# Splitting a spectral kernel's token transforms by even and odd frequency, with ScalarE statistics, a shorter filter product and new pacing costs

## The chip, the core and the metric

One core of a Trainium2 chip runs the whole program. The engines are TensorE (PE, with its weight loads PEld), VectorE (DVE), ScalarE (ACT), GpSimd (POOL) and SyncE (SP, which issues the transfers). Each engine works through its own instructions in order; they meet at semaphores. The metric is the time of one execution on the device, in microseconds (us).

## What is computed

With x of 2048 tokens by 448 features, the output is x plus two branches on its layer norm: a spectral filter over both axes and a gated network of 1792 hidden columns.

```python
xn = _layernorm(x, axis=-1)
# A: X = rfft2(xn, axes=(-2, -1));  X = X * (w_r + 1j * w_i);  y = irfft2(X, s=(S, D))
# B: gate = xn @ W_gate;  up = xn @ W_up;  h = gate * (gate > 0) * up;  h @ W_down
return x + _A_ref(xn, A_w_r, A_w_i) + _B_ref(xn, B_W_gate, B_W_up, B_W_down)
```

S is 2048 and D is 448. Products are kept close to float32 by splitting each operand into a float16 high and low part: three passes (high by high, high by low, low by high) stand for one product.

## The kernel before

**The gated network** takes most of TensorE. Token sets q = 0, 2, 1, 3 of 512 tokens each meet the 14 hidden blocks in groups of 5, 5 and 4. One gate unit (`gu_unit`) is 20 full passes of 128x128 by 512 and a share of four half passes on 64 rows (`gu_halves`) that open the banks of the next unit. Behind it come `gu_relu` (ScalarE, L966), `gu_times` (VectorE, L970), `gu_hi` (ScalarE, L974) and `gu_lo` (VectorE, L978). A down unit (`dn_mm`) is 12 or 15 passes of 448 columns, seeded and read back by ScalarE.

**The spectral branch** runs in the background between these units. Tokens are n = 16 n1 + n2: a transform over n1 (128 points) by a matrix, and one over n2 (16 points) by butterflies on VectorE. Forward, for each pair (a, a + 8) of n2: `f_dft` (feature transform, 48 passes on 64 rows), eviction to `eo` by ScalarE (L479), `f_a` and `f_b` (VectorE), `f_hi` (ScalarE) and `f_lo` (VectorE) for the split, `f_sdft` (token transform, three passes of 128x128 by 464 for each n2), `f_y1` (first butterfly), then the later stages. The filter takes each block's mirror image by a transfer (`swap`), adds it (`pair`) and multiplies by the weights (`wmul`, four full-width and four half-width VectorE operations for two blocks: L621, L624, L626, L627, counting both). Backward, a round p = 0 to 7 for each pair (p, p + 8): `i_join` (L515 to L735), `i_swap`, `i_pair` (L661, L662), `i_mix` in two halves (L418 to L441), `i_hi` (ScalarE, L765), `i_lo` (VectorE, L770), `i_sdft` (12 passes of 128x128 by 128 for each n2), `i_pqhi` (ScalarE, L784), `i_pqlo` (VectorE, L787), `i_ddft` (48 passes on 64 rows, with x seeded by ScalarE, L798, and read back, L814).

**Statistics.** `ln_stats` takes mean and variance of a chunk of 128 tokens with VectorE's batch norm operations; chunks of sets 1 and 3 do so in the background (`ln_chunk`), then `ln_norm` on ScalarE, `ln_lo` on VectorE, and `ln_dma`, which transposes the tokens into the tile T of the set by a transfer.

**PSUM.** Two "gu" tiles of two banks, two "dn" banks, and two "fx" banks for all jobs of the spectral branch.

**What sets the order.** The opening is written out by hand (`OPENING`). After it, the list `bg` holds the background steps, each with a cost in us of VectorE time (`add`); `run_bg` takes as many at a unit as fit into a share of the unit's time (`room`, `load`), where `PE_US` and `V_US` give costs of TensorE jobs and of weight preparation. `offer` puts an `f_dft` or `i_ddft` up to stand behind a unit's half passes, if 6 us of units have gone by since; `force` places it if not. Passes of a job are tied together (`chained`), and later passes stand behind the last job taken that way (`state["bar"]`). A list scheduler then fixes each engine's order.

```python
    def offer(fn, *a):
        state["job"] = (state["at"], fn, a, 6.0)
```

## Time and profile before

| | before |
|---|---|
| median of 3 runs | 439.57 us (439.55 to 439.62) |
| span of the profiled execution | 438.4 us |
| TensorE busy | 430.9 us |
| VectorE busy | 371.2 us |
| ScalarE busy | 256.8 us |
| GpSimd busy | 36.4 us |
| transfers | 39.53 MB, mean 90 GB/s |

The profiled execution's own time is known as its span; the median of the timed runs is 1.2 us longer. A profile row gives the line, the engine, the operation, what is written and read, partitions by elements, the count, the busy time in us and the mean length in ns. Lengths of neighbouring operations of one engine overlap a little, so the distance from start to start in a timeline is the better price of one. A busy TensorE is not TensorE at its peak.

### The profile page before, as it was taken

How to read it: one execution, taken by the hardware profiler on the slowest of the kernel's cores; microseconds unless marked ns; L12 is line 12 of the kernel's file. 1: busy time of each engine (PE TensorE's matmuls, PEld its weight loads, DVE VectorE, ACT ScalarE, POOL GpSimd, SP SyncE). 2: the span in 40 equal slices, each digit the busy share in tenths (PEclk: the TensorE clock that was granted, in tenths of full speed). 3: DMA queues.
4: the chain of work that ended last, by engine and by line, in shares of the span. 5: the costliest groups of instructions: out<-in, count | busy, mean ns of one | idle time of the engine just before them, and what ended most of it. 6: DMA issues, size and time to landing. Idle time of an engine off the chain costs nothing.

```text
span 438.4 us, 8109 instructions
## 1 busy us (share of the span) xinstructions
PE 430.9 (98%) x3014; PEld 209.9 (48%) x3014; DVE 371.2 (85%) x916; ACT 256.8 (59%) x519; POOL 36.4 (8%) x72
## 2 busy tenths in 40 slices
PE   6999999999999999999999999999999999999997
PEld 2644544454444444444444444444554555554544
DVE  5998798999967999899999999698989978976213
ACT  5897494486357856625413675574565665756620
POOL 1140040033300040000000011000000000000000
PEclk9999999999999999999999999999999999999999
DMA  8769992042000363530402100020111121301112
GB/s 261 253 164 304 384 236 65 2 80 31 3 0 2 133 198 119 163 120 24 144 13 86 43 1 1 2 81 7 55 45 53 47 67 56 119 24 50 43 42 84
DMA packets 37720, 39.53 MB, mean 90 GB/s; under 512 B 17952, under 2 KB 32576, under 8 KB 37680
## 3 DMA queue, kind: packets, MB, share of 16 engines
q1 hardware_dynamic: 37680, 39.01, 29.3%
q8 instruction: 23, 0.38, 0.4%
q14 instruction: 17, 0.14, 0.1%
HBM read 24.25 MB, written 3.67 MB: 64 GB/s over the span
## 4 chain that ended last, share of the span: by engine, by line
PE 97%; ACT 1%; DMA 1%; DVE 0%; issue 0%; SPq 0%
PE gu L450 59%; PE dn L450 27%; PE fx L450 7%; PE dn L1034 1%; PE gu L1034 1%; DMA y<-in_xr 1%; ACT tt L330 1%; ACT junk L192 0%; PE fx L406 0%; PE fx L1034 0%; ACT y L321 0%; DVE bst L265 0%; ACT rs L282 0%; PE gu L384 0%; DVE xy L1013 0%
## 5 line engine op out<-in xcount | busy, mean ns | idle before, releaser
L450 PE MATMUL gu<-T,wt 128*128 128x512 f16 (+2 forms) x1250 | 269.6, 376 | 0.0
L450 PEld LDWEIGHTS <-wt 128*128 128x128 f16 (+1 forms) x1250 | 111.7, 97 | 141.4 <-issue 19.9
L450 PE MATMUL dn<-wdt,h 128*128 128x448 f16 x624 | 126.8, 353 | 0.0
L450 PEld LDWEIGHTS <-h 128*128 128x128 f16 x624 | 60.2, 98 | 57.3 <-issue 0.4
L974 ACT ACTIVATE h<-g 128x512 f16<-128x512 f32 x56 | 35.1, 626 | 61.4 <-DVE g L970 61.3
L970 DVE SCALAR_TENSOR_TENSOR g<-gu,g 128x512 f32<-128x512 f32 x56 | 38.5, 687 | 21.0 <-ACT g L966 20.9
L966 ACT ACTIVATE g<-gu 128x512 f32<-128x512 f32 x56 | 33.0, 590 | 35.4 <-PE gu L450 35.4
L1006 ACT ACTIVATE xy<-dn,dsc 128x448 f32<-128x448 f32 x44 | 27.6, 627 | 28.0 <-PE dn L450 27.9
L978 DVE TENSOR_TENSOR h<-g,h 128x512 f16<-128x512 f32 x56 | 38.4, 687 | 5.5 <-ACT h L974 5.5
L995 ACT ACTIVATE dn<-xy,dinv 128x448 f32<-128x448 f32 x44 | 27.8, 632 | 0.6
L195 POOL PARTITION_ALL_REDUCE wm<-wm x15 | 13.8, 929 | 170.5 <-ACT junk L192 170.5
L866 DVE SCALAR_TENSOR_TENSOR wt<-wst,wsc,wt 128x512 f16<-128x512 f32 x28 | 20.4, 747 | 3.8 <-ACT wt L862 3.8
L862 ACT ACTIVATE wt<-wst,wsc 128x512 f16<-128x512 f32 x28 | 19.2, 715 | 1.0 <-DVE wsc L202 0.9
L787 DVE SCALAR_TENSOR_TENSOR wf<-fx,wf 128x512 f16<-128x512 f32 x16 | 10.8, 690 | 8.9 <-ACT wf L784 8.9
L192 ACT ACTIVATE junk<-wst 128x512 bf16<-128x512 f32 x28 | 17.4, 623 | 1.3 <-DMA wst<-in_wgu 1.1
L784 ACT ACTIVATE wf<-fx 128x512 f16<-128x512 f32 x16 | 9.5, 597 | 9.8 <-PE fx L450 9.2
L814 ACT ACTIVATE xy<-fx,fsc 128x448 f32<-128x448 f32 x16 | 9.2, 629 | 9.4 <-PE fx L450 9.4
L527 DVE TENSOR_TENSOR y<-y,y 128x464 f32<-128x464 f32 x21 | 13.4, 639 | 0.2
L528 DVE TENSOR_TENSOR y<-y,y 128x464 f32<-128x464 f32 x21 | 13.4, 637 | 0.0
L265 DVE BATCH_NORM_STATS2 bst<-y 128x6 f32<-128x448 f32 x16 | 9.3, 621 | 4.4 <-DMA y<-in_xr 4.4
L770 DVE SCALAR_TENSOR_TENSOR vt<-wst,fsc,vt 128x464 f16<-128x464 f32 x16 | 10.5, 701 | 2.9 <-ACT vt L765 2.9
L450 PEld LDWEIGHTS <-vt 128*128 128x128 f16 x192 | 11.5, 98 | 1.9
(159 smaller groups left out, 489.5 us busy)
## 6 DMA issues: line engine op xcount, KB each, us to landing
wst<-in_wgu SPq DMA_DIRECT2D x28, 256.0 KB
wf<-in_wf SPq DMA_DIRECT2D x16, 232.0 KB
sw<-y SPq DMA_DIRECT2D x32, 114.2 KB
sw<-wst SPq DMA_DIRECT2D x16, 228.4 KB
y<-in_xr SPq DMA_DIRECT2D x16, 224.0 KB
xy<-in_x SPq DMA_DIRECT2D x16, 224.0 KB
out<-xy SPq DMA_DIRECT2D x15, 224.0 KB
wdst<-in_wd SPq DMA_DIRECT2D x14, 224.0 KB
```

The costliest lines, as they stand in the source:

```text
L192: A.activation(mt([128, 512], BF16, "junk")[:, 0:src.shape[-1]], src, AF.Square, scale=SQ, accum_out=acc)
L195: G.partition_all_reduce(o, i, 128, bass_isa.ReduceOp.add)
L450: r = P.matmul(*a, **k)
L527: V.tensor_tensor(t, a, b, op=OP.add)
L862: A.activation(w[:, 0:4, :], wst[f, g], AF.Copy, scale=wsc[f, g])
L866: V.scalar_tensor_tensor(w[:, 4:8, :], st, sc, w[:, 0:4, :], op0=OP.mult, op1=OP.subtract)
L966: last["A"] = A.activation(g1s[f, q], hps[f, q][:, 0, :], AF.Relu, scale=2.0 ** -22).ins
L970: last["V"] = V.scalar_tensor_tensor(g1, hps[f, q][:, 1, :], 2.0 ** -22, g1, op0=OP.mult, op1=OP.mult).ins
L974: A.activation(ht[f, q][:, 0, :], g1s[f, q], AF.Copy)
L978: V.tensor_tensor(h[:, 1, :], g1s.pop((f, q)), h[:, 0, :], op=OP.subtract)
L995: A.activation(dps[n2][:, 0:D], xy[n2], AF.Copy, scale=dinv[:, g:g + 1])
L1006: last["A"] = A.activation(xy[n2], dps[n2][:, 0:D], AF.Copy, scale=dsc[:, g:g + 1]).ins
```

## The change

- **Token transforms by even and odd.** Tokens are put in another order (`_tokens`), so that a partition block holds token halves n and n + 1024. `f_fold` on VectorE makes their sum and difference (the even and the odd frequencies) out of the banks of `f_dft`, with one half copied to SBUF by ScalarE first. `f_sdft` then takes 12 passes of 64 rows by 64 columns for a pair, and `i_sdft` 48 passes of 64 rows by 64 columns (128 weights). Backward, `i_part` (ScalarE) and `i_unfold` (VectorE) put the halves together ahead of `i_pqhi` and `i_pqlo`, which now is a plain subtraction.
- **fx** is one tile of two banks, not two tiles of one.
- **Statistics** of sets 1 and 3 go to ScalarE (`ln_sum`, `ln_var`); the last 64 columns of `ln_lo` are copied by ScalarE.
- **Filter product.** A third weight plane (a second copy of the imaginary part, one half negated by `wneg`) lets `wmul` take three full-width operations for a block.
- **Swaps** take four transfers for two, since the sine rows now stand in blocks of 32.
- **Costs** in the planner's tables are replaced, and `f_fold` and the forced `f_dft` stand ahead of `f_lo`.

```diff
+def _tokens():
+    b, p = np.arange(16)[None, :], np.arange(128)[:, None]
+    return (1024 * (b // 8) + 16 * (p % 64) + b % 8 + 8 * (p // 64)).reshape(-1)
...
+    def fx2():
+        return psum.tile([128, 2, 512], F32, name="fx", bufs=1)
...
-        V.bn_aggr(mv[q][:, j, :], bst.pop((q, j)))
+    def ln_sum(q, j):
+        A.activation(mt([128, 512], BF16, "junk")[:, 0:D], xr_t[q + 4 * j], AF.Copy, accum_out=mv[q][:, 0, j:j + 1])
+    def ln_var(q, j):
+        A.activation(mt([128, 512], BF16, "junk")[:, 0:D], xr_t[q + 4 * j], AF.Square, bias=mv[q][:, 1, j:j + 1],
+                     accum_out=mv[q][:, 2, j:j + 1])
...
-        for h in range(2):
-            with tc.high_priority(offset=400):
-                A.activation(F[:, 4 - 4 * h:8 - 4 * h].rearrange(...), banks[h][:, 0:2 * 4 * GW]..., AF.Copy,
+        t = fa[a] = free.pop(0)
+        with tc.high_priority(offset=400):
+            A.activation(t.rearrange("p (i s) c k -> p i (s c k)", i=2), ps[:, :, 0:4 * GW], AF.Copy,
+                         scale=2.0 ** -14)
+    def f_fold(a):
+        ps = fps.pop(a)[:, :, 4 * GW:8 * GW].rearrange("p i (x k) -> p i x k", k=KC)
+        for b in range(2):
+            V.scalar_tensor_tensor(F[:, b], ps, (-1.0) ** b * 2.0 ** -14, t, op0=OP.mult, op1=OP.add)
...
-    def f_sdft(n2):
-        for i, (a, b) in enumerate(((0, 0), (0, 1), (1, 0))):
-            mm(y, m[:, a, :], xh[:, b], start=(i == 0), stop=(i == 2), skip_group_check=True)
+    def f_sdft(a):
+        for i, (x, y) in enumerate(((0, 0), (0, 1), (1, 0))):
+            for k in range(2):
+                for b in range(2):
+                    p, q = slice(64 * k, 64 * k + 64), slice(64 * b, 64 * b + 64)
+                        m = chained(mm(ps[q, k, 0:XW], w[p, b, x], xh[p, y], start=(i == 0), stop=(i == 2),
...
+        for k2, x, t in ts:
+            V.tensor_tensor(t, x, ws[k2][:, 0, :, None, :].to_broadcast([128, NG, 2, KC]), op=OP.mult)
+        for k2, x, t in ts:
+            V.tensor_tensor(x, x, ws[k2][:, 1:3].rearrange("p c g k -> p g c k"), op=OP.mult)
+        for k2, x, t in ts:
+            V.tensor_tensor(t, t, x[:, :, ::-1], op=OP.add)
...
+    def i_sdft(p):
+        for b in range(2):
+            for g in range(4):
+                o = slice(64 * (2 * g + b), 64 * (2 * g + b + 1))
+                for i, (h, c) in enumerate(((0, 0), (0, 1), (1, 0))):
+                    for e in range(2):
+                        q = slice(64 * e, 64 * e + 64)
+                            m = chained(mm(ps[:, e, o], v[q, h, 128 * g:128 * (g + 1)], w[q, c],
+    def i_part(p):
+        A.activation(yu[p][:, 1], sps[p][:, 0], AF.Copy, scale=2.0 ** -14)
+    def i_unfold(p):
+        for b in range(2):
+            V.scalar_tensor_tensor(y[:, b], ps[:, 1], (-1.0) ** b * 2.0 ** -14, y[:, 1], op0=OP.mult, op1=OP.add)
+    def i_pqhi(p):
+        A.activation(t[:, 0], yu[p], AF.Copy)
+    def i_pqlo(p):
+        for b in range(2):
+            V.tensor_tensor(pgh[p + 8 * b][:, 1], y[:, b], pgh[p + 8 * b][:, 0], op=OP.subtract)
...
-    PE_US = {"f_dft": 0.85, "f_sdft": 0.59, "i_sdft": 0.65, "i_ddft": 0.82, "row_dft": 0.2}
+    PE_US = {"f_dft": 0.85, "f_sdft": 0.75, "i_sdft": 0.85, "i_ddft": 0.82, "row_dft": 0.2}
...
-    bf = (1.09, 1.74, 1.74, 1.74, 1.22, 1.74, 1.74, 1.74)
+    bf = (1.28, 2.07, 2.07, 2.07, 1.58, 2.07, 2.07, 2.07)
...
-        add(2.14, f_b, a)
+        add(3.02, f_b, a)
...
         if k < 7:
             add(0.0, force, f_dft, seq[k + 1], seq[k + 1] + 8)
+            add(1.27, f_fold, seq[k + 1])
         for n2 in (a, a + 8):
-            add(0.0, f_sdft, n2)
+            add(0.64, f_lo, a, n2)
+        add(0.0, f_sdft, a)
...
         if p:
-            both(0.6, i_pqlo, p - 1)
+            add(1.3, i_pqlo, p - 1)
             add(0.0, offer, i_ddft, p - 1, p + 7)
...
-            add(1.99, i_mix, p + 1, 0)
-    both(0.6, i_pqlo, 7)
+            add(1.28, i_pair, p + 1)
+        add(1.38, i_unfold, p)
+        add(0.0, i_pqhi, p)
+        if p < 7:
+            add(2.32, i_mix, p + 1, 0)
+    add(1.3, i_pqlo, 7)
...
-    V_US = {"w_scale": 0.2, "w_lo": 0.66, "wd_scale": 1.1, "wd_lo": 0.6}
+    V_US = {"w_scale": 0.33, "w_lo": 0.75, "wd_scale": 1.9, "wd_lo": 0.69}
...
-        c = 1.2 if units[i][0] == "gu" else 0.0
+        c = 1.37 if units[i][0] == "gu" else 0.0
```

**TensorE, fifth inverse round (p = 4).** In the program before, fx_4521 and fx_4534 are the two i_sdft of the round, fx_4644 and fx_4645 the banks of its i_ddft, gu_4601 a gate unit and dn_4746 a down unit; wf holds the split result between the two transforms. Before:

```order
L450 MATMUL fx_4534<-im_4204,vt_2350 128x128
L450 LDWEIGHTS wt_3560
L450 MATMUL gu_4601<-T1_64,wt_3560 128x512
...
L450 MATMUL dn_4746<-wdt_3713,h_4177 128x448
L450 LDWEIGHTS wf_4547
L450 MATMUL fx_4645<-idc_t_84,wf_4547 128x56
L450 LDWEIGHTS wf_4547
L450 MATMUL fx_4644<-idc_t_84,wf_4547 128x56
```

Gate and down passes stood between the two transforms. The same place in the changed kernel, where fx_4633 is i_sdft(4), fx_4808 is i_ddft(4), and gu_4782 and gu_4803 are a pair of gate units (line 495 is the line of every pass there):

```order
L495 LDWEIGHTS wt_3577
L495 MATMUL gu_4782<-T1_64,wt_3577 128x512
L495 LDWEIGHTS vt_2418
L495 MATMUL fx_4633<-im_4286,vt_2418 128x64
...
L495 LDWEIGHTS wf_4688
L495 MATMUL fx_4808<-idc_t_84,wf_4688 128x56
...
L495 LDWEIGHTS wt_3624
L495 MATMUL gu_4803<-T1_64,wt_3624 128x512
```

Before, 24 gate passes and 7 down passes stood between the two transforms of the round; now the last pass of i_sdft(4) is followed at once by the first of i_ddft(4), and the 20 full passes of gu_4803 stand behind it.

**VectorE at the same place.** Before, from the gate unit's operations to i_pqlo (L787) of the two n2 and the second half of i_mix:

```order
L978 TENSOR_TENSOR h_4577<-g1_4574,h_4577 128x512
L422 TENSOR_TENSOR wst_4239<-wst_4553 128x3x116
L423 TENSOR_TENSOR wst_4239<-wst_4553 128x3x116
L787 SCALAR_TENSOR_TENSOR wf_4547<-fx_4521,wf_4547 128x512
L787 SCALAR_TENSOR_TENSOR wf_4549<-fx_4534,wf_4549 128x512
L435 TENSOR_TENSOR wst_4239<-wst_4239 128x116
```

The two L787 came behind the whole first half of i_mix. In the changed kernel, where L853 is i_unfold, L463 to L468 the first half of i_mix and L863 i_pqlo:

```order
L1046 SCALAR_TENSOR_TENSOR g1_4925<-gu_4782,g1_4925 128x512
L1054 TENSOR_TENSOR h_4928<-g1_4925,h_4928 128x512
L853 SCALAR_TENSOR_TENSOR wf_4682<-fx_4633,wf_4682 128x512 x2
L463 TENSOR_TENSOR wst_4690<-wst_4331 128x2x232
L465 TENSOR_TENSOR wst_4690<-wst_4331 128x2x2x116
L467 TENSOR_TENSOR wst_4331<-wst_4690 128x3x116
L468 TENSOR_TENSOR wst_4331<-wst_4690 128x3x116
L863 TENSOR_TENSOR wf_4688<-wf_4682,wf_4688 128x512 x2
```

Two operations stood between i_sdft and the operands of i_ddft; now it is four, with the first half of the next round's i_mix between them and the gate unit's two ahead of them.

**ScalarE, statistics of the third token set.** In the changed kernel L302 is ln_sum, L308 ln_var, L313 the root, L391 the high part and L406 the copy of its last 64 columns. The rows from the last sum to the root:

```order
L302 ACTIVATE junk_984,ms_977<-y5_71 128x448
L1071 ACTIVATE dn_1447<-xy_61,dinv_92 128x448
L1042 ACTIVATE g1_1032<-gu_933 128x512
L308 ACTIVATE junk_987,ms_977<-y16_82,ms_977 128x448
L389 ACTIVATE y0_66<-y16_82,ms_977 128x448
...
L308 ACTIVATE junk_993,ms_977<-y5_71,ms_977 128x448
L503 ACTIVATE fx_878<-eps_93 128x1
L313 ACTIVATE rt_995<-ms_977,eps_93 128x4
```

These rows put all eight statistics passes and the four subtractions of the mean (L389) ahead of the root. Before, the first high part (L348) stood five rows behind the root (L282), and no statistics on this engine:

```order
L282 ACTIVATE rs_955<-mv_944,eps_93 128x4
L346 ACTIVATE y14_80<-y16_82,rs_955 128x448
L995 ACTIVATE dn_831<-xy_61,dinv_92 128x448
L497 ACTIVATE Xh_754<-eo_718 128x464
L497 ACTIVATE Xh_756<-eo_718 128x464
L348 ACTIVATE tt0_101<-y14_80,rs_955 128x448
```

The statistics have come from VectorE's queue into ScalarE's, ahead of the root, and the gate unit's L1042 now stands among them.

## The prediction

> **What bounds the kernel now.** I read the page first (span, busy times, chain), then the TensorE groups by shape, then timelines of one forward and one inverse round, engine by engine.

> ```profile
> span 438.4 us, 8109 instructions
> PE 430.9 (98%) x3014; PEld 209.9 (48%) x3014; DVE 371.2 (85%) x916; ACT 256.8 (59%) x519; POOL 36.4 (8%) x72
> PE 97%; ACT 1%; DMA 1%; DVE 0%; issue 0%; SPq 0%
> ```

> TensorE is the bound: 97% of the chain that ended last. After the opening it never stands, so every pass taken out shortens the run, and every new wait of TensorE lengthens it by its full length. VectorE is busy 371.2 of 438.4 us without being waited for. The first question is thus how much TensorE work goes, the second whether VectorE and ScalarE still deliver before TensorE asks.

> **TensorE work.** Rows of the groups by shape (count | busy, mean ns), then of the timeline (start, length, operation, count):

> ```profile
> L450 PE MATMUL fx<-im,vt 128*128 128x128 f16 x192 | 12.2, 219 | 0.0
> L450 PE MATMUL fx<-Xh,fm 128*128 128x464 f16 x48 | 11.2, 359 | 0.0
> L406 PE MATMUL fx<-id_t,tt 128*64 128x128 f16 x24 | 1.4, 246 | 0.0
> ...
> 68.97 0.82 PE L450 MATMUL fx<-fd_t,T 64*128 64x58 f16 x48
> 69.73 4.70 PE L450 MATMUL gu<-T,wt 128*128 128x512 f16 x22
> 74.27 1.34 PE L450 MATMUL fx<-Xh,fm 128*128 128x464 f16 x6
> 75.44 0.81 PE L450 MATMUL gu<-T,wt 128*128 128x512 f16 x3
> ...
> 354.16 1.50 PE L450 MATMUL fx<-im,vt 128*128 128x128 f16 x24
> 355.50 0.35 PE L450 MATMUL dn<-wdt,h 128*128 128x448 f16 x1
> ...
> 362.15 0.79 PE L450 MATMUL fx<-idc_t,wf 64*128 64x56 f16 x48
> 362.87 1.47 PE L450 MATMUL gu<-T,wt 128*128 128x512 f16 x6
> ```

> Start to start, the six forward passes of a pair cost 75.44 - 74.27 = 1.17 us (0.195 us per 464 columns, 0.42 ns a column), the 24 inverse ones 1.34 us. The 64-row passes show what halving does: 48 passes of 56 columns cost 0.72 us, 48 of 58 cost 0.76. Two run at once, so 24 x 56 x 0.42 ns = 0.56 us is work and 0.16 us the price of going in and out of the half-array form.
> - f_sdft becomes 12 passes of 64 rows by 64 columns, four at once: 3 x 0.195 + 0.16 = 0.75 us, saving 0.42 us a pair, 3.4 us in eight pairs. That column halves run together the trace shows only in the opening: 24 transposes of 128x64 are busy 1.4 us, 0.06 us each at a mean of 246 ns. Without it f_sdft costs 6 x 0.195 + 0.16 = 1.33 us and loses 1.3 us in all.
> - i_sdft becomes 48 passes of 64 rows and 64 columns, two at once: 24 x 64 x 0.42 ns + 0.16 = 0.80 us, saving 0.54 us, 4.3 us in eight.

> Together **-7.7 us**, with bounds of -3.0 (columns not together) and -8.5 (the 0.16 us shared with the neighbouring half passes).

> [...]

> **Vector and Scalar work.** Mean ns of the operations that come and go:

> ```profile
> L265 DVE BATCH_NORM_STATS2 bst<-y 128x6 f32<-128x448 f32 x16 | 9.3, 621 | 4.4 <-DMA y<-in_xr 4.4
> L627 DVE TENSOR_TENSOR y<-y,y 128x232 f32<-128x232 f32 x16 | 6.4, 397 | 0.0
> L556 DVE TENSOR_TENSOR y<-y,fx 128x464 f32<-128x464 f32 x8 | 5.0, 631 | 0.0
> L192 ACT ACTIVATE junk<-wdst 128x448 bf16<-128x448 f32 x14 | 7.9, 566 | 0.1
> L192 ACT ACTIVATION_READ_ACCUMULATOR junk<-wdst 128x1 f32 x14 | 2.6, 189 | 0.0
> ```

> VectorE gains f_fold (16 x 0.63 = 10.1 us) and 16 subtractions of 512 in i_pqlo (16 x 0.69 = 11.0, the length of the like L978 row below). It loses eight L265 (5.0 us), and the filter trades 32 half-width additions (12.7) for 16 full ones (10.1): +13 us of busy time, about 384 us. ScalarE gains 16 statistics passes of 0.566 + 0.189 us (12.1 us) and 8 copies of 1024 columns. In sum this costs nothing where TensorE is far behind; the cover is some microseconds in each round. Moving f_fold ahead of f_lo puts f_lo, and behind it f_sdft, after the f_dft of the next pair; 69.73 + 4.54 = 74.27 shows that TensorE does 4.5 us of gate work between these two, more than the copy and the two operations of f_fold (0.6 + 1.3), so nothing there. The single two-bank fx tile has the same cover. SP issues 56 more transfers:

> ```profile
> 208.86 0.88 SPq L609 DMA_DIRECT2D wf<-in_wf  x2
> 213.40 0.73 SPq L653 DMA_DIRECT2D sw<-y  x1
> ```

> A filter step would hold 8 issues of at most 0.73 and 4 of 0.44 us, 7.6 us, and SP stands from 209.7 to 213.4 between two steps; nothing, or where SP's queue fills, up to 1 us.

> **The place that decides: the fifth inverse round (p = 4).** The built order of the changed kernel puts i_ddft(4) straight behind i_sdft(4). Before, 24 gate and 7 down passes stood between them, about 6 us. i_ddft(4) reads what comes out of i_sdft(4) by way of ScalarE (i_part), VectorE (i_unfold), ScalarE (i_pqhi) and VectorE (i_pqlo), so TensorE must now wait for this whole chain. Its durations, from one round of before (VectorE, then ScalarE):

> ```profile
> 350.40 0.64 DVE L418 TENSOR_TENSOR wst<-wst 128x464 f32<-128x464 f32 x1
> ...
> 352.06 0.52 DVE L423 TENSOR_TENSOR wst<-wst 128x348 f32<-128x348 f32 x1
> 355.66 1.36 DVE L787 SCALAR_TENSOR_TENSOR wf<-fx,wf 128x512 f16<-128x512 f32 x2 [3.08 <-ACT wf L784]
> 356.94 0.27 DVE L435 TENSOR_TENSOR wst<-wst 128x116 f32<-128x116 f32 x1
> ...
> 359.32 0.39 DVE L515 SCALAR_TENSOR_TENSOR y<-y 128x232 f32<-128x232 f32 x1
> ...
> 359.94 0.69 DVE L970 SCALAR_TENSOR_TENSOR g<-gu,g 128x512 f32<-128x512 f32 x1
> 360.54 0.63 DVE L734 SCALAR_TENSOR_TENSOR wst<-y,y 128x464 f32<-128x464 f32 x1
> ...
> 361.64 1.31 DVE L770 SCALAR_TENSOR_TENSOR vt<-wst,fsc,vt 128x464 f16<-128x464 f32 x2
> 362.87 0.64 DVE L661 TENSOR_TENSOR wst<-wst,sw 128x464 f32<-128x464 f32 x1
> ...
> 363.97 0.69 DVE L978 TENSOR_TENSOR h<-g,h 128x512 f16<-128x512 f32 x1
> ...
> 355.03 1.27 ACT L784 ACTIVATE wf<-fx 128x512 f16<-128x512 f32 x2 [1.45 <-PE fx L450]
> ...
> 359.44 1.10 ACT L765 ACTIVATE vt<-wst,fsc 128x928 f16<-128x928 f32 x1 [0.47 <-DVE wst L441]
> 360.66 0.63 ACT L974 ACTIVATE h<-g 128x512 f16<-128x512 f32 x1
> 361.50 0.60 ACT L966 ACTIVATE g<-gu 128x512 f32<-128x512 f32 x1 [0.20 <-PE gu L450]
> ```

> Start to start on VectorE: first half of i_mix 352.06 - 350.40 + 0.44, less a hole of 0.1: 2.0 us; i_unfold 1.3 (as the two L787); second half 2.2 (356.94 to 359.32 has holes); i_join 0.62 + 1.10; gu_times 0.60, gu_lo 0.60; i_lo 1.23; i_pair 1.10; i_pqlo 1.2 (two like L978).

> *First wait.* Count from the end of the gate unit ahead of i_sdft(3). TensorE is through i_sdft(3), 37 gate passes of 0.216 (512 x 0.42 ns), i_ddft(3) and four half passes after 0.5 + 0.8 + 8.0 + 0.7 + 0.6 = 10.6 us, and asks for i_sdft(4). VectorE in its order: gu_times ends at 1.3 (0.65 behind ScalarE's L966), gu_lo at 2.65 (L974 between), i_unfold 3.95, i_mix 5.95, i_pqlo 7.15, second half 9.35, gu_times and gu_lo 10.55, i_join 12.25, i_lo(4) 13.5. TensorE waits 2.9 us.

> *Second wait.* i_sdft(4) ends at 14.3. VectorE: i_pair 14.6, gu_times 15.2; ScalarE's L974 15.9, then i_part 16.5, while gu_lo also ends at 16.5; i_unfold 17.8, i_mix 19.8 (ScalarE's i_pqhi, 1.10 x 1024/928 = 1.2 us, is done at 19.1), i_pqlo 21.0. TensorE stands from 14.3 to 21.0, 6.7 us. Queued behind the waiting pass are all later gate and down passes; SP and ScalarE are not held.

> Both: **+9.6 us**. Bounds: the bare chain, 0.6 + 1.3 + 1.2 + 1.2 = 4.3 us, and 12 us if VectorE enters the round 2.5 us late. I take 9.6, as the queues stand in the order.

> **The clock behind it.**

> ```profile
> 1.88 5.31 PE L1294 MATMUL dn<-bw 128*128 128x512 f16 x16 [1.88 <-POOL bw L1366]
> ...
> 433.83 1.31 PE L1034 MATMUL fx<-wdt,h 128*128 128x224 f16 x12
> ...
> 438.40:440.00 1.60, 0.00 (x0) 0.63 0.00 0
> ```

> TensorE's last pass ends at 433.83 + 1.31 = 435.14 us. In the window behind the span the granted clock (0.63, a mean over 1.6 us) has left 1.00; if it fell to one half, it did so at 438.8. So some 3.7 us of standing are enough, and 6.7 us fall into it. What a cold start costs the opening shows: 16 passes take 5.31 us and not 16 x 0.216 + 0.15 = 3.6: **+1.7 us**. Bounds 0 and, if it stays cold twice as long, 3.4.

> **The third token set.**

> ```profile
> 58.20 8.49 SPq L373 DMA_TRANSPOSE T<-tt  x4
> 78.60 1.67 PE L450 MATMUL gu<-T,wt 128*128 128x512 f16 x7
> ```

> The set's transposes are issued by 66.7 us and TensorE first needs them at 78.60: 12 us of cover. Now ScalarE does eight passes of 0.755 us (6.0 us), the squares wait for the mean on VectorE, and all four high parts (4 x 0.56) and low parts (4 x 0.6) stand behind the root; four issues of 1.4 us follow the first low part. That moves the last issue by 6.0 + 2.2 + about 3 of hand-overs, to 78, with the landing behind it. The cover is used up: **+1.0 us**, between 0 and 3.

> **Sum.** -7.7 + 9.6 + 1.7 + 1.0 = +4.6 us: the span goes from 438.4 to 443.0. The runs shown have a median of 439.57, 1.2 us over this execution's span; with the same 1.2 us I predict **444.2 us**.

> **Rivals.**
> - *VectorE is not behind at p = 4 (faster).* Then the first wait goes and the second shrinks to the bare chain of 4.3 us, too short a stand to bring the clock down for certain: 439.6 - 7.7 + 4.3 + 1.0 = 437.2. It decides at 5.8 us of waits in all: below that the change is faster by more than can be told from none (7.7 - 1.0 - 0.9). For it: before, VectorE itself waited 3.08 us ahead of L787 in such a round. Against: the round now asks 13.5 us of VectorE where TensorE gives 10.6. Chance 0.10.
> - *The clock holds* through the waits: 444.2 - 1.7 = 442.5. For it: 3.7 us is read off one fall at the end. Chance 0.13.
> - *VectorE is late elsewhere too*: 384 us of work in 443, with 8 weight halves and 2 statistics sets in the same queue; a second wait of 2 to 4 us makes 447. For it: the waits of L770 and L978 have little room. Against: no wait at 371 us of work. Chance 0.12.
> - *The change does not do what it says*: columns do not run together, saving 3.0: 448.9. Against: the opening's 0.06 us. Chance 0.04.
> - [...] Chance 0.03. [...]

> **How the numbers follow.** The forecast has 0.58; its own bounds run from 440 (both waits at their least, no late set) to 447. The range leaves out the ends of small chance, the first rival's 437.2 and 448.9: 439.0 to 447.5. About 0.2% (0.9 us) can be told from no change here. Faster by more: 0.11 (the first rival and a little of short waits); within: 0.08 (low ends of the forecast and of the clock's rival); slower: 0.81.

> **What would show it.** Passes of fx<-Xh,fm and fx<-im,vt: 0.75 and 0.80 us a pair in the timeline. A TensorE hole of about 3 us before, and one of 6 to 7 us behind, the fifth group of fx<-im,vt, near 365 us, ended by VectorE's i_pqlo; a window behind it with granted clock 0.5 for some 3.4 us; a hole of about 1 us ended by a DMA near 80 us. I am wrong if TensorE is still unbroken there, or if other holes add up to more.

## The result and the profile after

| | before | changed |
|---|---|---|
| median | 439.6 us (439.55 to 439.62) | 500.4 us (499.25 to 500.53) |
| span of the profiled execution | 438.4 us | 498.4 us |

The ratio is 1.138 (95% interval 1.136 to 1.139): 61 us slower, where 4.6 were forecast. The page of the changed kernel: the busy times, rows of the 40 slices of 12.5 us, and the chain that ended last by engine and by line.

```profile
span 498.4 us, 8711 instructions
PE 439.2 (88%) x3254; PEld 205.1 (41%) x3254; DVE 384.0 (77%) x908; ACT 269.4 (54%) x551; POOL 31.1 (6%) x72
...
PE   6999998899999999388669956994999995699997
...
DVE  6995877779999896565789568993998879986513
...
PEclk9999999999999999879889985999899999699999
...
DVE 33%; PE 25%; DMA 21%; ACT 9%; issue 5%; SPq 4%; POOL 1%; DVEq 0%; ACTq 0%; POOLq 0%
PE gu L495 14%; DMA sw<-y 12%; PE dn L495 7%; DMA y<-in_xr 3%; DVE g L1046 3%; DVE h L1054 3%; DMA wst<-in_wgu 2%; PE fx L495 2%; DMA xy<-in_x 2%; SPq L712 2%; DVE y L681 2%; DVE y L588 2%; DVE wt L942 1%; DVE y L587 1%; DVE y L603 1%
```

VectorE's busy time is what the prediction said (384), TensorE works in 88% of the span and not in 98%, and the chain is no longer TensorE's: it runs through VectorE and through a transfer, sw<-y, the swap of the filter. TensorE's row is nearly whole up to the sixteenth slice (two 8s between 75 and 100 us); the holes are in slices 17 to 28 (200 to 350 us), which is the filter and the start of the inverse rounds, and in 34 and 35, the fifth inverse round. TensorE's, then VectorE's and ScalarE's largest waits (line, what for: us in total, times, longest):

```profile
PE gu L495 <- DVE g L1046: 28.1, 7, 10.5
PE dn L495 <- ACT h L1050: 8.3, 1, 8.3
PE fx L495 <- ACT fx L874: 6.2, 1, 6.2
PE dn L495 <- ACT dn L1071: 2.4, 2, 1.3
PE fx L495 <- ACT xy L890: 2.4, 1, 2.4
PE gu L495 <- DMA T<-tt: 2.1, 1, 2.1
...
DVE y L719 <- DMA sw<-y: 29.0, 11, 3.7
...
ACT wf L675 <- DMA wf<-in_wf: 34.8, 9, 9.6
```

TensorE's two waits for fx (6.2 and 2.4) are those of the fifth inverse round, the one for T (2.1) is the late token set: the forecast's own. The first two rows, 36 us, are not in it. Behind them VectorE waits in `pair` (L719) for the swap, and ScalarE in `wneg` (L675) for the filter weights, and in both queues a gate unit's operations stand behind the waiting one. One place of each kind in the timeline (start, length, engine, operation; idle before it and what ended that), VectorE's first:

```profile
198.61 11.41 SPq L712 DMA_DIRECT2D sw<-y  x10
...
201.07 2.05 PE L495 MATMUL dn<-wdt,h 128*128 128x448 f16 x10
203.45 0.40 DVE L719 TENSOR_TENSOR y<-y,sw 128x232 f32<-128x232 f32 x1 [3.12 <-DMA sw<-y]
...
208.27 0.40 DVE L719 TENSOR_TENSOR y<-y,sw 128x232 f32<-128x232 f32 x1 [3.00 <-DMA sw<-y]
...
210.00 0.68 DVE L1046 SCALAR_TENSOR_TENSOR g<-gu,g 128x512 f32<-128x512 f32 x1
...
210.72 0.63 ACT L1050 ACTIVATE h<-g 128x512 f16<-128x512 f32 x1 [13.27 <-DVE g L1046]
...
211.40 2.04 PE L495 MATMUL dn<-wdt,h 128*128 128x448 f16 x5 [8.27 <-ACT h L1050]
...
233.25 0.40 ACT L675 ACTIVATE wf<-wf 128x232 f32<-128x232 f32 x1 [9.60 <-DMA wf<-in_wf]
233.55 0.58 ACT L1042 ACTIVATE g<-gu 128x512 f32<-128x512 f32 x1
```

SP needs 11.4 us for ten swap issues; VectorE gets two blocks 4.8 us apart, `gu_times` (L1046) stands behind both, and TensorE stands 8.3 us for its h. At 233 us it is ScalarE that waits, in `wneg`, with `gu_relu` (L1042) behind. Ahead of this SP had been issuing swaps without a pause. The same stretch of SP's queue in the kernel before (two transfers of 63 rows a swap; the first and the last of twelve issues in 9.7 us, 0.81 us each), then in the changed one (four of 31 and 32 rows):

```profile
173.15 0.87 SPq L653 DMA_DIRECT2D sw<-y  x1
...
182.16 0.71 SPq L654 DMA_DIRECT2D sw<-y  x1
```

```profile
185.92 24.10 SPq L712 DMA_DIRECT2D sw<-y  x24
```

24 issues in 24.1 us, 4.9 us a swap in its later part, while a single issue takes 0.6 us: SP waits between them. Its transfers raise eight semaphores in turn (in this trace each of the 275 behind the first eight raises that of the transfer eight issues back), and an issue waits for the landing of that one: those at 193.01, 195.71 and 197.98 us start behind landings at 192.99, 195.64 and 197.96 us. The trace holds the signals by which a transfer's landing is counted, and they point to the cause. By rows of the transfer: signals for each, and median time from the start of the issue to the last signal:

```
kernel           transfer                rows  signals  to the last signal
before           swap, filter              63       10  2.8 to 2.9 us
changed          swap, filter              31        2  7.5 us
changed          swap, filter              32       16  8.1 us
changed          swap, inverse             31        2  11.2 us
before           weights, two planes      128       16  3.4 us
changed          weights, two planes      128       16  6.3 us
```

A transfer of 31 rows has two signals where one of 32 has 16. In the six swaps from 185.92 us on, the last signals of the 31-row transfers come one behind another, 2.3 to 2.7 us apart (190.72, 192.99, 195.64, 197.96, 200.60 us and on), those of the 32-row transfers 0.2 us each behind them. The packets of the trace, one for each row, agree: of the first swap the first eleven start one behind another, each when the one ahead of it has ended, from 187.20 to 188.50 us; in the kernel before, of the 126 of the first swap's two transfers, 23 start within 0.25 us and 100 in the same time. This is read here as 31 rows going to one data engine, on which the 32-row transfers and the weights then queue too: the load issued at 210.39 us has its first signal at 212.57 us and its last at 218.57, 0.25 us behind the last of the swaps. That it is one engine, and why with 31 rows, is not shown: no packet of the trace says which engine carried it. An estimate from the trace: between 188 and 210 us a packet of 1856 bytes (one row) takes 78 ns in the median; a swap's 31 + 31 rows one behind another take 62 x 78 ns = 4.8 us, near the 4.9 us a swap above.

### The profile page after: what moved, and what is told of

The parts are those of the page before. It is cut to its first block, busy times and chain, and to the rows that moved or that the text cites. A ratio compares the mean times of both kernels' runs of the same rounds, so it can differ in the third digit from the quotient of the medians.

```text
span 498.4 us, 8711 instructions
## 1 busy us (share of the span) xinstructions
PE 439.2 (88%) x3254; PEld 205.1 (41%) x3254; DVE 384.0 (77%) x908; ACT 269.4 (54%) x551; POOL 31.1 (6%) x72
## 4 chain that ended last, share of the span: by engine, by line
DVE 33%; PE 25%; DMA 21%; ACT 9%; issue 5%; SPq 4%; POOL 1%; DVEq 0%; ACTq 0%; POOLq 0%
PE gu L495 14%; DMA sw<-y 12%; PE dn L495 7%; DMA y<-in_xr 3%; DVE g L1046 3%; DVE h L1054 3%; DMA wst<-in_wgu 2%; PE fx L495 2%; DMA xy<-in_x 2%; SPq L712 2%; DVE y L681 2%; DVE y L588 2%; DVE wt L942 1%; DVE y L587 1%; DVE y L603 1%
## 5 line engine op out<-in xcount | busy, mean ns | idle before, releaser
L495 PE MATMUL gu<-T,wt 128*128 128x512 f16 (+2 forms) x1250 | 278.6, 387 | 30.2 <-DVE g L1046 28.1
L495 PEld LDWEIGHTS <-wt 128*128 128x128 f16 (+1 forms) x1250 | 113.9, 99 | 181.1 <-issue 66.0
L495 PE MATMUL dn<-wdt,h 128*128 128x448 f16 x624 | 128.9, 356 | 12.3 <-ACT h L1050 8.3
L1046 DVE SCALAR_TENSOR_TENSOR g<-gu,g 128x512 f32<-128x512 f32 x56 | 38.3, 683 | 20.5 <-ACT g L1042 20.2
L1042 ACT ACTIVATE g<-gu 128x512 f32<-128x512 f32 x56 | 32.8, 586 | 17.3 <-PE gu L495 17.3
L719 DVE TENSOR_TENSOR y<-y,sw 128x232 f32<-128x232 f32 x16 | 6.4, 399 | 37.5 <-DMA sw<-y 29.0
L1082 ACT ACTIVATE xy<-dn,dsc 128x448 f32<-128x448 f32 x44 | 27.1, 623 | 10.6 <-PE dn L495 10.2
L1071 ACT ACTIVATE dn<-xy,dinv 128x448 f32<-128x448 f32 x44 | 27.4, 630 | 0.6
L675 ACT ACTIVATE wf<-wf 128x232 f32<-128x232 f32 x16 | 6.3, 394 | 34.9 <-DMA wf<-in_wf 34.8
L223 POOL PARTITION_ALL_REDUCE wm<-wm x15 | 9.0, 599 | 190.6 <-ACT junk L220 190.6
L534 DVE SCALAR_TENSOR_TENSOR eo<-fx,y 128x464 f32<-128x464 f32 x16 | 9.5, 631 | 8.3 <-ACT y L523 8.3
L823 ACT ACTIVATE vt<-wst,fsc 128x928 f16<-128x928 f32 x8 | 8.8, 1101 | 10.5 <-DVE wst L486 10.5
L874 ACT ACTIVATE fx<-xy,fsc 128x448 f32<-128x448 f32 x16 | 10.1, 628 | 7.9 <-DVE wf L853 7.8
L587 DVE TENSOR_TENSOR y<-y,y 128x464 f32<-128x464 f32 x21 | 13.3, 635 | 0.1
L588 DVE TENSOR_TENSOR y<-y,y 128x464 f32<-128x464 f32 x21 | 13.3, 634 | 0.1
L550 ACT ACTIVATE Xh<-eo 128x464 f16<-128x464 f32 x16 | 8.8, 594 | 8.2 <-DVE eo L486 8.0
```

The costliest lines, as they stand in the source:

```text
L495: r = P.matmul(*a, **k)
L587: V.tensor_tensor(t, a, b, op=OP.add)
L588: V.tensor_tensor(d, a, b, op=OP.subtract)
L1042: last["A"] = A.activation(g1s[f, q], hps[f, q][:, 0, :], AF.Relu, scale=2.0 ** -22).ins
L1046: last["V"] = V.scalar_tensor_tensor(g1, hps[f, q][:, 1, :], 2.0 ** -22, g1, op0=OP.mult, op1=OP.mult).ins
L1071: A.activation(dps[n2][:, 0:D], xy[n2], AF.Copy, scale=dinv[:, g:g + 1])
```

## The experiments

Theory A is the above. The rivals: B, the number of transfers and SP's time to issue them; C, the weights (three pairs of buffers for six single ones, a third plane loaded); D, VectorE has too much work.

**1. Wide swaps in the changed kernel.** Rows 0 and 32 are carried along, and GpSimd sets them to zero again.

```diff
-PAIRS = ((slice(1, 32), slice(33, 64)), (slice(33, 64), slice(1, 32)), (slice(64, 96), slice(96, 128)),
+PAIRS = ((slice(0, 32), slice(32, 64)), (slice(32, 64), slice(0, 32)), (slice(64, 96), slice(96, 128)),
...
         for o, i in PAIRS:
             nc.sync.dma_start(t[o], cur[key][i])
+        for r in (0, ROW): G.memset(t[r:r + 1], 0.0)
```

> The changed kernel with its swaps in transfers of 32 rows: the two of 31 rows (1 to 31 and 33 to 63) also carry rows 32 and 0, which GpSimd then sets to zero again; the number of transfers (four) and TensorE's order are as in the changed kernel. Theory A (a transfer of 31 rows is carried by one data engine, since its landing counts 2 signals where 63 rows count 10 and 32 rows 16; the swaps land in 7 to 8 us instead of 2.9, and SP, with eight transfers under way, stands): swaps land in about 3 us, TensorE's waits of 28 us for g and 8 us for h go, and the run takes what the forecast's other terms leave, 440 to 448 us. Rival B (the number of transfers and their issue time, 2.6 us a swap instead of 1.5): hardly better than the changed kernel, over 480. Rival C (three pairs of weight buffers instead of six single ones, an extra load a block): over 480, ScalarE still waits some 30 us for the weights. Rival D (VectorE has too much work, 384 us): over 470, TensorE waits for VectorE with the swaps landed.

454.5 us (454.39 to 455.55), ratio to the kernel before 1.034 (1.032 to 1.036). Its SP queue at the same place, the busy times, and TensorE's largest waits:

```profile
186.12 16.23 SPq L712 DMA_DIRECT2D sw<-y  x24
...
PE 429.2 (95%) x3254; PEld 203.1 (45%) x3254; DVE 383.3 (85%) x908; ACT 268.2 (59%) x551; POOL 61.0 (13%) x120
...
PE fx L495 <- ACT fx L874: 5.9, 1, 5.9
PE gu L495 <- DVE g L1046: 2.8, 3, 1.8
PE fx L495 <- ACT xy L890: 2.4, 1, 2.4
PE dn L495 <- ACT dn L1071: 2.4, 2, 1.4
PE gu L495 <- DMA T<-tt: 2.2, 1, 2.2
```

All swaps have 16 signals and land in 2.0 us (filter) and 2.2 us (inverse). The same number of issues now take 16.2 us. 46 of the 61 us are gone, and TensorE, VectorE and ScalarE work through the same instructions in the same order; 36 us of TensorE's waits became 3. Not all of the 46 us was waiting: TensorE's busy time for the same passes fell by 10.0 us (439.2 to 429.2), since 26.5 us of it ran at half clock in the changed kernel and 7.2 us here (the last section shows when the clock falls). A is right by far on what the landings cost. It leaves 454.5, above the 440 to 448 expected, so the forecast's other terms are some 10 us short; 5 to 7 answer that.

**2. Six wide transfers.** Rows 15 + 16 + 15 + 16 + 32 + 32, no zeroing.

```diff
+PAIRS = ((slice(1, 16), slice(33, 48)), (slice(16, 32), slice(48, 64)), (slice(33, 48), slice(1, 16)),
+         (slice(48, 64), slice(16, 32)), (slice(64, 96), slice(96, 128)), (slice(96, 128), slice(64, 96)))
```

> The changed kernel with each swap in six transfers of 15, 16 and 32 rows instead of four of 31 and 32: the same bytes, no zeroing, more transfers. Theory A: 15 rows go over several data engines, so the run comes near that with four wide transfers, within 5 us of it, although SP issues two more a swap (3.7 us a swap). Rival B (number of transfers): slower than the changed kernel, 505 to 530. Rivals C and D: as the changed kernel, 500.

461.6 us (1.050, 1.048 to 1.052); 15 rows have 16 signals and land in 2.1 us. Wide again, and far from the 505 to 530 of B; but 7 us behind the four, more than the 5 expected. ScalarE's wait for the weights is 31.9 us against 13.3 in experiment 1: the loads stand behind 4.0 us of issues a swap. B may have a small share, once there are six; how large is not shown, since the order of TensorE's passes is another from the filter on.

**3 and 4. The kernel before with four transfers a swap**, cut behind 33 rows (3, shown) or behind 32 (4, with 33 and 97 in CUT):

```diff
-        nc.sync.dma_start(t[1:64], cur[key][65:128])
-        nc.sync.dma_start(t[65:128], cur[key][1:64])
+CUT = ((1, 34), (34, 64), (65, 98), (98, 128))
...
+        for l, h in CUT:
+            nc.sync.dma_start(t[l:h], cur[key][(l + 64) % 128:(h + 63) % 128 + 1])
```

> The kernel before with each swap in four transfers (33, 30, 33 and 30 rows) instead of two of 63: prices the number of transfers alone. Theory A: landing near 3 us, 439.5 to 442. Rival B: SP's issue time, 24 x 1.0 us more, shows as 450 or more. Rivals C and D: 440.

> The kernel before with each swap in four transfers of 32 and 31 rows: the same number and bytes as with 33 and 30. Theory A: the two of 31 rows run on one data engine, landing goes to 7 or 8 us as in the changed kernel, and the old kernel slows to 460 to 500. Rival B: as with 33 and 30 rows, within 2 us. Rivals C and D: 440, since weight buffers and VectorE's work are the old ones.

33 and 30 rows: 439.6 us, ratio 1.000 (0.999 to 1.001). 32 and 31 rows: 469.8 us, 1.069 (1.067 to 1.071). SP's queue in the first, then in the second, with the second's largest waits of TensorE and VectorE:

```profile
172.94 20.14 SPq L654 DMA_DIRECT2D sw<-y  x24
```

```profile
172.86 23.65 SPq L654 DMA_DIRECT2D sw<-y  x24
...
PE gu L450 <- DVE g L970: 17.7, 5, 5.6
...
DVE y L661 <- DMA sw<-y: 23.6, 8, 4.3
```

33, 30 and 31 rows have 12, 16 and 2 signals and land in 2.1, 2.1 and 8.6 us. One row to the other side of the cut costs 30 us in a kernel without any other part of the change: 3 and 4 have the same instructions in the same order on TensorE, VectorE and ScalarE, so theory A stands alone, and twice as many transfers, which also land sooner (2.1 us against 2.8 to 2.9), cost nothing in sum (against B).

**5 to 7. What else was short.** On top of the wide swaps: the offer of i_ddft moved behind the second half of i_mix (5), the statistics of sets 1 and 3 back on VectorE (6), and both (7).

```diff
-            add(0.0, offer, i_ddft, p - 1, p + 7)
...
         add(3.02, i_mix, p, 1)
+        if p: add(0.0, offer, i_ddft, p - 1, p + 7)
```

```diff
+        elif q in CHUNKS[2:]: V.tensor_scalar(nm, m[:, :, 0], -1.0, None, op0=OP.mult)
...
-            add(0.0, ln_sum, q, j)
-        add(0.17, ln_mean, q)
-        for j in range(4):
-            add(0.0, ln_var, q, j)
-        add(0.0, ln_root, q)
-        add(0.65, ln_inv, q)
+            add(0.63, lambda q, j: (ln_bn(q, j), ln_ag(q, j)), q, j)
+        add(0.0, ln_sd, q)
+        add(0.6, lambda q: [ln_r(s, q) for s in "abcde"], q)
```

> The changed kernel with the four wide transfers, and i_ddft offered to the planner only behind the second half of i_mix instead of ahead of it: TensorE's order is the same up to the third inverse round; from there on 37 gate and 3 down passes stand between every i_sdft and its i_ddft, in the fifth round too. The forecast's central term (first wait 2.9, second wait 6.7, cold clock 1.7 us at the fifth round; in the run with wide transfers the waits were 2.4 and 5.9 us and the clock 0.5 until 387.5 us, together some 11 us) says: 454.5 - 11 = 443 to 445 us, no wait over 1 us behind 360 us. Rival D (VectorE has too much work in any order): the waits move to other rounds and the run stays over 450.

> The changed kernel with the four wide transfers, and the statistics of sets 1 and 3 back on VectorE (batch norm operations) instead of the two passes a chunk on ScalarE. The forecast's term for the late token set, mis-sized at 1.0: the wait of 2.2 us for the third set near 80 us and the one of 1.4 us near 97 us (a down pass waiting for ScalarE's L1071, behind the statistics of the last set) both go: 450 to 452 us. Rival (the statistics were put there because VectorE lacks the 4 us): waits for VectorE in the filter stage grow by as much, 454 us or more.

> Both of these together. If the terms add up: 454.5 - 11 - 3.5 = 440 us, near the kernel before, since some 5 us of waits between 200 and 305 us are left and the passes save 7. Rival D: over 448.

443.2 us (1.008, 1.006 to 1.009), 451.6 us (1.027, 1.025 to 1.029) and 440.2 us (1.001, 1.000 to 1.002). Against experiment 1 that is -11.3, -3.0 and -14.3: the two add up. In 5 no wait over 1 us is left behind 360 us, in 6 those near 80 and 97 us are gone. TensorE's largest waits left in 7 behind the opening (lines count one higher here) are all that remains of D:

```profile
PE gu L496 <- DVE g L1047: 2.6, 3, 1.1
...
PE dn L496 <- ACT dn L1072: 1.7, 2, 1.5
```

In 7 neither transform is broken by a wait, so it measures the passes: summed start to start over the run, f_sdft takes 3.4 us less than before and i_sdft 4.3 us less, 7.7 together. That leaves out the way in: the full pass just ahead of passes on 64 rows takes 0.10 us longer (a gate pass 0.31 for 0.22 us, a down pass 0.28 for 0.19), which the 128-row transforms of before did not cost (0.22 and 0.19 us ahead of them). In 7 this happens 18 times, 1.7 us, so 6.0 us are saved; TensorE's whole busy time fell by 4.9 (430.9 to 426.0), and the rest was not traced.

**8. The narrow transfers issued by GpSimd**, in the filter and the inverse rounds.

```diff
-            nc.sync.dma_start(t[o], cur[key][i])
+            nc.gpsimd.dma_start(t[o], cur[key][i])
```

> The changed kernel with its swaps in the same four transfers of 31 and 32 rows, issued by GpSimd instead of SP. Theory A asks on how many data engines they run: if GpSimd's transfers of 31 rows are spread, landing is 2 to 4 us, and with SP free of 96 issues the run takes 445 to 458; if they keep to one engine, it stays at 480 to 505. Rival B (SP's issue time) says 445 to 460 in either case, with the landing still at 7 us.

455.7 us (1.037, 1.035 to 1.039). From this queue the 31 rows have 16 signals, and in the filter they land in 1.9 us. So it is not the 31 rows as such: from SP's queue the same ones land in 7.5 us (changed kernel), and what the two queues do differently is not shown. Without any zeroing, and with another order of TensorE's passes from the filter on, the run ends beside experiment 1.

**9 to 11. Towards a version below both.** 8 with both edits of 7 (9); the same with the old filter product (10, two weight planes loaded, four half-wide for two full-wide operations in two blocks); 9 with `wneg` put one step later (11).

```diff
         for k in pair_k:
-            add(0.79, pair, ("X", k), 1)
+            add(0.0, wneg, k); add(0.79, pair, ("X", k), 1)
...
-        for k in (ks[i0 - 1], ks[i0 - 1] + 8) if 0 < i0 < 9 else ():
-            add(0.0, wneg, k)
```

> All three together: swaps of 31 and 32 rows issued by GpSimd (landing 1.9 us in the run before, no zeroing), i_ddft offered behind the second half of i_mix, statistics on VectorE. In the run with zeroed wide swaps, the late offer and these statistics (440.2 us) TensorE still had about 5.5 us of waits between 185 and 302 us, of which the two near 300 us (2.4) stand behind GpSimd's zeroing of the inverse swaps. If that is so: 437 to 439 us, the first version below the kernel before. Rival: the waits belong to VectorE's work, which is larger than before by some 17 us with these statistics: 440 or more.

> As the one with all three, and the filter product as before: two weight planes loaded instead of three, two full-width and two half-width VectorE operations a block instead of three full-width ones. By the rows, a block costs VectorE 2 x 0.63 + 2 x 0.40 = 2.06 us instead of 1.90, and SP issues 16 loads of 116 KB less. The forecast's theory (VectorE not waited for in the filter, SP with room): within 1 us of the one with all three. Rival C (the third plane's loads are late and hold ScalarE): 2 us or more faster.

> The version with all three, and ScalarE's negation of a weight half (wneg) put at the head of the step that multiplies by it, one step later than before. In the version with all three, ScalarE stood 8.9 us in six waits for the weights' loads, with the down units' seeds (L1072) and relu queued behind, and TensorE waited 1.4 us for such a seed near 186 us. If the weights' loads are what holds ScalarE there: this wait goes and the run takes 437 to 439 us. Rival (the seed is late because of ScalarE's other work there, squares and weight preparation): 439.5 to 440.5, and VectorE's multiplication waits for ScalarE instead.

9 took 439.8 us (1.000, 0.999 to 1.001), above the range expected: the later of the two waits near 300 us went, as GpSimd's zeroing was gone, and TensorE's waits behind the opening fell from 4.3 us in 7 to 2.9; but the order changed from 200 us on, and TensorE's busy time rose from 426.0 to 427.2, for a cause that stays open. 10 took 441.4 us (1.004, 1.002 to 1.005), 1.6 us more than 9, over the 1 us allowed and with the other sign than C. That the three-operation product saves this is not shown: the order differs from 201 us on, and behind a wait of 2.3 us near 296 us the clock was down for 3.4 us. In the one run of five whose mean granted clock was 0.999 and not 0.995, 10 took 440.2 us. 11 took 438.8 us, ratio 0.998 (0.997 to 0.999): the only version below the kernel before. Its span and busy times, and TensorE's largest wait behind the opening:

```profile
span 437.0 us, 8744 instructions
PE 426.4 (98%) x3254; PEld 201.8 (46%) x3254; DVE 387.8 (89%) x924; ACT 256.4 (59%) x519; POOL 82.7 (19%) x168
...
PE gu L496 <- DVE g L1047: 1.8, 2, 1.4
```

ScalarE's 8.9 us of waits for the weights and TensorE's wait for a seed, both there in 9, are gone, as expected; the order differs from 208 us on, so how much of the 1.0 us is due to them is not shown.

## Why the prediction was wrong, step by step

The direction held, the size did not: 500.4 us against 444.2 and a range to 447.5. The direction was not luck: with wide swaps the change is still 15 us slower, most of it in the fifth inverse round, as forecast. The range was narrower than the prediction's own bounds: with the second wait at 4.3, no first wait, 1.7 for the clock and no late set the sum is 437.9, with 12, 3.4 and 3 it is 450.3, where it says 440 and 447. The result lies far outside either.

- **The step that failed** is "SP issues 56 more transfers ... nothing, or where SP's queue fills, up to 1 us". It priced a transfer by its issue, from rows of 63-row transfers, and gave no bound for the landing of a transfer of another shape; 31 rows were not in the trace of before, and the nearest rows did not bound them. Measured by experiment 1: 46 us in the changed kernel, 30 us in the old one (4 against 3). The way to TensorE is the one in the timeline above: swap, VectorE's `pair`, behind it `gu_times`, and from there h and the down unit; and beside it weights, `wneg`, behind it ScalarE's `gu_relu`.
- **TensorE work**, -7.7: the two transforms themselves give 3.4 + 4.3 = 7.7, as forecast, but the way into passes on 64 rows takes back 1.7 (experiment 7). The 0.16 us that the prediction set for going in and out was read from the first pass of such a group on, so the way in is not in it. Columns do run together, so that rival falls: in the changed kernel the 12 passes of f_sdft take 0.71 us, where the forecast has 0.75. The 48 of i_sdft take 0.81 us for 0.80, two starting within 4 ns and the pairs 29 ns apart, for 64 x 0.42 = 27 ns of columns; a least time of a pass, to which the chance of 0.03 was given, no run shows.
- **The fifth inverse round**, 2.9 + 6.7: measured 2.4 and 6.2 in the changed kernel, at the place named, though the rows name other operations.

```profile
416.73 0.59 PE L495 MATMUL gu<-T,wt 64*128 64x512 f16 x4
418.51 1.14 ACT L890 ACTIVATE xy<-fx,fsc 128x448 f32<-128x448 f32 x2
419.23 1.31 DVE L828 SCALAR_TENSOR_TENSOR vt<-wst,fsc,vt 128x464 f16<-128x464 f32 x2
419.69 1.37 PE L495 MATMUL fx<-im,vt 64*128 64x64 f16 x48 [2.38 <-ACT xy L890]
427.24 0.28 PE L495 MATMUL fx<-idc_t,wf 64*128 64x56 f16 x4 [6.18 <-ACT fx L874]
427.70 1.25 PE L495 MATMUL fx<-idc_t,wf 64*128 64x56 f16 x44 [0.18 <-DVE wf L863]
```

  The first wait ends with ScalarE's read-back of the i_ddft before (L890) out of the one fx tile, which the prediction had put at nothing. The `i_lo` that it named (L828) holds the passes twice more inside their 1.37 us (0.87 us a round earlier), so a free fx tile would have gained nothing. With this 0.5 us the first wait is 2.9. The second ends with x's seed (L874), and four passes later the low parts of `i_pqlo` (L863) are the last to come, as forecast.

- **The clock behind it**, 1.7: mis-sized. The same place in experiment 1, where no cold stretch of the filter is near it:

```profile
374.44 1.65 PE L495 MATMUL fx<-im,vt 64*128 64x64 f16 x48 [2.44 <-ACT xy L890]
381.99 0.28 PE L495 MATMUL fx<-idc_t,wf 64*128 64x56 f16 x4 [5.90 <-ACT fx L874]
```

  TensorE restarts at 382.0 and the clock comes back at 387.7 us (below): 5.7 us at half speed lose 2.9 us, for 1.7. The 48 passes between the two waits run at half speed as well, but this costs little: they take 1.65 us, where the changed kernel, there still at full clock, takes 1.37, and the second wait is shorter by as much (5.90 for 6.18). With the 0.8 us by which they exceed 0.87 the place is worth 2.4 + 0.8 + 5.9 + 2.9 = 12.0 us; taking it out (experiment 5) brought 11.3.
- **The third token set**, 1.0: 2.1, and the same statistics cost once more near 97 us, where a down unit's seed (L1071) waits 1.4 us behind those of the last set. Putting them back brought 3.0.
- **VectorE's 13 us more** "costs nothing where TensorE is far behind": nearly. With the swaps wide, 4.4 us of waits for VectorE and ScalarE are left between 200 and 306 us; the rival that put 2 to 4 us on a late VectorE was the better step. A part of these is GpSimd's zeroing, which the changed kernel does not have.

So the gain did not fail to come: some 6 us were saved and some 67 lost, 46 of them to the two transfers of 31 rows in each swap.

## What to carry to other kernels

When a change gives a transfer another number of rows, look at when it will have landed and not only at how long its issue takes; on SP's queue here swaps of 33, 32 and 30 rows landed in 2.0 to 2.1 us in the filter (experiments 1 and 3) and of 31 in 7.5 to 8.6 (changed kernel, experiment 4), so a cut one row to the side was worth 30 us in one kernel, and the same transfers from another queue 45 us in the other. The late transfers reached TensorE because the engines that waited for them had its gate units' operations behind them in their queues; look there for the price of a late landing. Where one transform reads another's result by way of two other engines, keep other TensorE work between them: 40 passes hid the whole chain in experiment 5.

## What the hardware showed that was not expected

The granted clock in experiment 1 around the fifth inverse round (window, its length, TensorE busy with count, granted clock, share and GB/s of transfers). TensorE's last pass ahead of the first wait ends at 371.99 us:

```profile
371.50:372.00 0.50, 0.49 (x10) 1.00 0.00 0
...
373.50:374.00 0.50, 0.00 (x0) 1.00 0.00 0
374.00:374.50 0.50, 0.07 (x4) 0.58 0.00 0
...
381.50:382.00 0.50, 0.01 (x2) 0.50 0.00 0
...
387.00:387.50 0.50, 0.50 (x3) 0.50 0.13 43
387.50:388.00 0.50, 0.50 (x3) 0.77 0.03 3
```
